# Windowed attention and a routed mixture of experts: when the experts' matrices are loaded, and where the flag of the leftover pass is made

## Chip, cores and metric

One core of a Trainium2 chip. The metric is the device time of one execution in microseconds (us); several runs are made and their median is taken. Beside the runs there is one profiled execution, from which all views below come. Engines: PE is TensorE's matmul stream and PEld its weight loads, DVE is VectorE, ACT is ScalarE, POOL is GpSimd, SP is SyncE, which here issues the direct DMAs.

## The reference

Two blocks follow each other. The first is attention with 4 batches, 8 heads, 768 positions and head size 64, where a query sees the first `n_global` positions and a window of `n_local` (96) behind it, with a slope per head on the distance. The second is a mixture of 8 experts over the 3072 rows of 512 that come out, and each row goes to one expert:

```python
xn = x / (np.linalg.norm(x, axis=-1, keepdims=True) + 1e-06)
en = expert_emb / (np.linalg.norm(expert_emb, axis=-1, keepdims=True) + 1e-06)
logits = xn @ en.T / tau
expert_idx = np.argmax(logits, axis=1)
...                                     # softmax of logits; gate_w = the chosen expert's share
for e in range(E):
    mask = expert_idx == e
    h = np.maximum(x[mask] @ w1[e], 0.0)        # 512 -> 1024
    out[mask] = gate_w[mask, None] * (h @ w2[e])   # 1024 -> 512
```

All is in float32.

## The kernel before

**Attention, 0 to about 190 us.** Batches and heads go through in steps that are written out by hand; rows of the result go to DRAM, each row's expert is chosen on the way, and row numbers are scattered into one list for each expert. Nothing of this is changed, but that two small DVE operations of the flag (below) stood here in the order before.

**Experts, about 190 us to the end.** The order on every engine is written out by hand. A first piece (256 rows of expert 0) is started early. Then comes a loop over experts `e` = 0 to 7:

- `prepare(e + 1)` issues on POOL the four gathers of the next expert's rows (`xg`, L986) and, from expert 2 on, on SP the loads of that expert's matrices: `load_weights` (L167 for `w1`, L168 for `w2`, 2 MB each). There are two sets of buffers, so `w1` of expert e + 1 goes where that of expert e - 1 was.
- The scatters of the expert before (`out_dram`, L1247) are issued on POOL, then a POOL drain waits for them to land.
- `expert(e)`: all engines branch (a `Switch`, L1752) into the arm for the expert's number of rows. Of those arms only one runs. Inside, `first_by_seven` makes the first product with seven half-size products instead of eight (L1295 on PE, sums by L1307 on DVE); between the products, `fill` calls put other DVE work: `wsum` from this expert's `w2` (L1040 to L1043, two and two), and `fsum` and in-place sums from the *next* expert's `w1` (L1065, L1066), and the next rows' token sums (L1040, L1041 on `xT`). The list `spare` says which work goes to which of the six fills. Between products PE also transposes the next expert's rows (L1012). Then come the rows over 256 (`part_in_arm` L1241, `second_in_arm` L1228).
- Behind the arm, `Pair` makes the second product of the first 256 rows with seven products (L1102): `begin` has four of them with fills behind the second, third and fourth, `end` the other three. `begin`'s fills hold the rest of the next expert's sums (L1042, L1043, L1067, L1068) and, on each engine, the load of a later expert's width into a register (`take_width`, L1498). A hint for the next branch is given ahead of it (L1504).

Waits around the loads: SP's first load of an expert waits not only for its buffer but also for `k.out_again`, an operation of the `Pair` two experts before the loaded one. That is the ACT copy of the first product (L1127), or for expert 2 a DVE operation of expert 0's `end_apart`:

```python
self.k.out_again = nc.scalar.copy(out=self.p1, in_=m).ins
...
t.w = new_weights(n, (wp_a, n.wp_b)[e % 2])
wait_for(n, load_weights(n, e, t.w), [n.out_again])
```

**The leftover.** After the loop, `leftover` makes two flags: whether inputs are outside what the window code can do, and whether any expert has more than 512 rows left. A product with ones on PE (L1516) and five DVE operations give the flag `fi`, all engines load it into a register (L1525) and branch (L1526) past a long, general pass that does not run with these inputs.

Of the kernel before, what the change touches and what calls it, by code (L numbers as in the profile page):

```python
# [9 lines left out]
F32 = mybir.dt.float32  # L10
I32 = mybir.dt.int32
AF = mybir.ActivationFunctionType
ALU = mybir.AluOpType
# [7 lines left out]
P = 128  # L21
NEG = 1e9
CAP = 512
# [141 lines left out]
def load_weights(k, e, w):  # L165
    nc = k.nc
    first = nc.sync.dma_start(w[0][:], k.w1[e].rearrange("(c p) f -> p c f", p=P))  # L167
    nc.sync.dma_start(w[1][:], k.w2[e].rearrange("(f p) m -> p f m", p=P))  # L168
    return first
# [915 lines left out]
class Pair:  # L1085
# [13 lines left out]

    def product(self, ps, x, w, add=False):  # L1100
        for f in range(4):
            self.k.nc.tensor.matmul(ps, lhsT=x[:, f, :], rhs=w[:, f, :], start=f == 0 and not add, stop=True,  # L1102
                                    skip_group_check=True)

    def plus(self, out, x, z):
        self.k.nc.vector.tensor_tensor(out=out, in0=x, in1=z, op=ALU.add)  # L1106
# [3 lines left out]

    def last(self, i, out, x, z):

        return self.k.nc.vector.scalar_tensor_tensor(out=out, in0=x, scalar=self.gate[i], in1=z, op0=ALU.mult, op1=ALU.add)

    def scatter(self, i):
        return lambda: scatter_rows(self.k, self.y[i][:], self.ids[:, i, 1:2])

    def begin(self, split=False, spare=((), (), ())):

        def fill(i):  # L1120
            for make in spare[i]:
                make()

        nc, (t1, t2, t3, t4), (s1, s2, s3, s4) = self.k.nc, self.sums, self.left
        m = self.m = self.bank()
        self.product(m, self.a[0][0], self.b[0][0])
        self.k.out_again = nc.scalar.copy(out=self.p1, in_=m).ins  # L1127
        n = self.bank()
        self.product(n, s2, t2)
        self.plus(self.u2, n, self.p1)  # L1130
        nc.scalar.mul(self.u2g, self.u2, self.gate[0])
        fill(0)
        if split:
            self.fourth()
        n = self.bank()
        self.product(n, s3, t3)
        self.plus(self.u3, n, self.u2)
        nc.scalar.mul(self.u3g, self.u3, self.gate[1])
        fill(1)
        n = self.bank()  # L1140
        self.product(n, self.a[1][1], t4)
        self.last(1, self.part(1, 0), n, self.u3g)
        fill(2)
# [20 lines left out]
    def end_apart(self):  # L1164

        t1, (s1, s2, s3, s4) = self.sums[0], self.left
        n = self.bank()
        self.product(n, s1, t1)
        self.k.out_again = self.last(1, self.part(1, 1), n, self.u3g).ins
        self.last(0, self.u3, n, self.u2g)  # L1170
        n = self.bank()
        self.product(n, s4, self.b[1][1])
        self.last(0, self.part(0, 1), n, self.u3)
        return [self.scatter(0), self.scatter(1)]
# [83 lines left out]
def wait_for(k, i, others):  # L1258
    for x in others:
        k.tc.add_manual_dep(i.ins, x.name,  # L1260
                            mybir.DependencyInfo(mybir.DependencyClass.Sync, mybir.DependencyReason.DATA),
                            reason="it comes behind all of them")
# [75 lines left out]
def expert(k, now, coming, widths, unfinished):  # L1338


    tc = k.tc
    w1, w2 = now.w
    hT = new_hidden(k)
    if coming:
        coming.xT = new_turned(k)

    def between(f):
        at = {1: (0,), 2: (1,), 3: (2,), 4: (3,)} if now.e else {5: (0,), 6: (1, 2), 7: (3,)}
        for j in at.get(f, ()) if coming else ():
            turn_row(k, coming.rows, coming.xT, j, k.nc.scalar.copy)  # L1350

    a = [[hT[:, 4 * j : 4 * j + 4, i * P : (i + 1) * P] for j in range(2)] for i in range(2)]
    now.sums, spare = weight_sums(k, w2)
    left, making = hidden_sums(k, a)
    more, ahead = [], []
    if coming:
        coming.token_sums, more = token_sums(k, coming.xT)
        if now.e:
            coming.first_sums, ahead = first_sums(k, coming.w[0])
    spare = [spare[:2], spare[2:], ahead[:1], ahead[1:2], more[:2], []]  # L1360
    tiles = range(2 if now.e else 1, CAP // P)
    ps = None if now.e else k.work0.tile([P, k.DM], F32, name="work", tag="work")
    k.order = list(range(4, 8)) + list(range(4)) if now.e else list(range(8))
    steps = widths_of(now.e)
    for arm in tc.Switch(now.width.index, len(steps), hint=now.width.hint):
        w = steps[arm]
        if now.e:
            first_by_seven(k, now, hT, w, between, list(spare))
            for make in making:
                make()  # L1370
        else:
            first_by_eight(k, now.xT, w1, hT, w, between)
        for size in (32, 64):
            if w % (2 * size) >= size:
                part_in_arm(k, now, hT, w2, w // (2 * size) * 2 * size, size)
        for j in tiles:
            if j < w // P:
                second_in_arm(k, now, hT, w2, j)
        if ps:
            second(k, ps, hT, w2, range(k.NF // 2))  # L1380

    def scatters():
        for j in tiles:
            scatter_rows(k, now.y[:, j - 1, :], now.tile_ids[:, j : j + 1])
        for size in (64, 32):
            scatter_rows(k, now.y_part[size][:], now.parts[size][0], P // size)

    def choose_next():
        if coming:
            give_hint(k, coming.e, widths[coming.e])  # L1390

    out = [scatters]
    if now.e:
        pair = Pair(k, now.rows, a, left, w2, now.sums)
        choose_next()
        out += unfinished.pop()()
        number = [lambda: widths.append(take_width(k, now.e + 2))] if now.e + 2 < k.E else []
        pair.begin(spare=(more[2:], number + ahead[2:3], ahead[3:]))
        ps = k.work0.tile([P, k.DM], F32, name="work", tag="work")
        unfinished.append(pair.end(ps[:, 0:256]))  # L1400
        out.append(pair.scatter(1))
    else:
        choose_next()
        widths.append(take_width(k, 2))
        out += unfinished.pop()()
        for make in more:
            make()
        second(k, ps, hT, w2, range(k.NF // 2, k.NF))
        unfinished.append(lambda: end_second(k, now.rows, ps))
    return out  # L1410
# [82 lines left out]
def take_width(k, e):  # L1493

    t = Net()
    n = len(widths_of(e))
    engines = ARMS if e else ARMS[:2]
    v = k.nc.values_load(k.pick[0:1, e : e + 1], engines=engines, min_val=0, max_val=n - 1)  # L1498
    t.index, t.hint = {eng: v for eng in engines}, "expert%d" % e
    return t  # L1500
# [3 lines left out]
    k.tc.switch_hint(t.index, len(widths_of(e)), t.hint)  # L1504


def leftover(k):


    nc, tc, E = k.nc, k.tc, k.E  # L1510
    passes = -(-k.N // CAP)
    more = passes - 1
    flags = k.const.tile([P, 2], F32, name="flags")
    ps = k.work.tile([P, 512], F32, name="work", tag="work")
    nc.vector.tensor_tensor(out=k.good[:], in0=k.good[:], in1=k.fits[:], op=ALU.mult)
    nc.tensor.matmul(ps[:, 0:1], lhsT=k.ones[:], rhs=k.good[:], start=True, stop=True)  # L1516
# [1 line left out]
                            op0=ALU.is_lt)  # L1518
# [1 line left out]
    nc.vector.tensor_reduce(out=most[:], in_=k.need[:], op=ALU.max, axis=AX.X)  # L1520
    nc.vector.tensor_scalar(out=flags[:, 1:2], in0=most[:], scalar1=float(CAP), scalar2=flags[:, 0:1],
                            op0=ALU.is_gt, op1=ALU.max)
    fi = k.const.tile([P, 2], I32, name="fi")
    nc.vector.tensor_copy(out=fi[:], in_=flags[:])
    any_ = nc.values_load(fi[0:1, 1:2], min_val=0, max_val=1)  # L1525
    with tc.If(any_ > 0):  # L1526

        wait_for(k, nc.sync.dma_start(k.i_dram[0:1, 0:2], fi[0:1, :]), k.outs)
        redo = nc.values_load(fi[0:1, 0:1], min_val=0, max_val=1)
# [7 lines left out]
        with ExitStack() as inner:  # L1537
# [15 lines left out]
            with tc.For_i(0, E * passes, 1) as i:  # L1553
# [3 lines left out]
                with tc.If(n > 0):  # L1557
                    e = i // passes
# [16 lines left out]
def kernel(  # L1575
# [13 lines left out]
    n = Net()  # L1589
# [26 lines left out]
    with ExitStack() as moe:  # L1616
# [43 lines left out]
        def prepare(e):  # L1660
            t = Net()
            t.e = e
            t.y, t.y_part = ys[e % 2]
            xgs, t.gathers = gather_rows(n, n.ids[:, e], n.xgp)
            t.rows = n.mt[:, e], n.ids[:, e], xgs
            if e < 2:
                t.w = n.w[e]
            else:
                t.w = new_weights(n, (wp_a, n.wp_b)[e % 2])
                wait_for(n, load_weights(n, e, t.w), [n.out_again])  # L1670
            return t

        with tc.manual_schedule(engines=ORDERED | set(ARMS) | {mybir.EngineType.Pool}):
# [37 lines left out]
            for e in range(n.E):  # L1711
                now, coming = coming, None
                parts_of(n, now)
                now.width = widths[e]
                if e == 1:
                    now.first_sums = first
                if e + 1 < n.E:
                    coming = prepare(e + 1)
                for scatter in pending:
                    scatter()  # L1720

                nc.gpsimd.drain()
                pending = expert(n, now, coming, widths, unfinished)
# [33 lines left out]
```

## Time and profile before

| | |
|---|---|
| Median of 5 runs | 523.28 us (521.61 to 524.31) |
| The profiled execution's own time | 523.07 us |
| Its span, first to last instruction | 521.3 us |
| PE busy | 497.4 us, 95% of the span |
| DVE, ACT, POOL busy | 302.4, 197.4, 152.0 us |
| Mean granted clock of PE | 0.99 |
| Instruction queue q8 | 63 packets, 1.03 MB |
| `w1t` loads of 2 MB | 6, landing 9.3 us after issue (median) |
| `w2t` loads of 2 MB | 6, landing 11.2 us after issue (median) |

The span lies inside the execution's time. "Idle before" in a row is the engine's own idle time ahead of an instruction, with the one that ended it; "issue" there means that the profile shows nothing that it waited for. A `q` behind an engine's name means its sequencer, which runs branches, register loads and waits. [...]

### The profile page before, as it was taken

The page shows a single profiled execution, that of the slowest core. Times are in us where ns is not written, and L with a number is a line of the kernel's source. Part 1 is how long each engine was busy: PE and PEld are TensorE (multiplying, and loading weights), DVE is VectorE, ACT ScalarE, POOL GpSimd, SP SyncE. Part 2 cuts the span into 40 slices and gives each one's busy share as a digit, 9 for nine tenths or more (in the row PEclk, how much of TensorE's full clock was granted, in tenths as well). Part 3 has the DMA queues.
Part 4 walks back from the last instruction along what each step waited for, and adds up shares of the span by engine and source line. Part 5 has one row for each costly group of instructions (what it writes and reads, how often), then busy time and mean ns, then how long its engine had stood idle before and what let it go on. Part 6 is the DMA issues. An engine that isn't in the chain of part 4 may idle for free.

```text
span 521.3 us, 13699 instructions
## 1 busy us (share of the span) xinstructions
PE 497.4 (95%) x5606; PEld 410.3 (79%) x5606; DVE 302.4 (58%) x601; ACT 197.4 (38%) x494; POOL 152.0 (29%) x169
## 2 busy tenths in 40 slices
PE   7999999999989898999989999999999999999994
PEld 6677787786767687788868669989899689869963
DVE  5656667776785665639625516746647554615531
ACT  4866776776744311313212221322323222311210
POOL 4221221152355335533430034054033040022031
PEclk9999999999998999999989999999999999999998
DMA  9999998988533627776480028257075073001002
GB/s 173 199 197 180 219 238 187 217 207 210 149 83 112 143 37 193 217 250 203 152 304 4 3 73 313 105 212 248 4 245 213 4 253 133 2 25 58 0 22 68
DMA packets 111422, 76.32 MB, mean 146 GB/s; under 512 B 87078, under 2 KB 95270, under 8 KB 111282
## 3 DMA queue, kind: packets, MB, share of 16 engines
q1 hardware_dynamic: 102769, 59.00, 42.9%
q0 software_dynamic: 6912, 15.26, 9.1%
q8 instruction: 63, 1.03, 0.9%
q14 instruction: 78, 0.63, 0.4%
q10 hardware_dynamic: 1600, 0.39, 0.3%
HBM read 61.66 MB, written 17.16 MB: 151 GB/s over the span
## 4 chain that ended last, share of the span: by engine, by line
PE 80%; DVE 5%; issue 4%; ACT 4%; DMA 3%; POOL 2%; SPq 1%; POOLq 0%; ACTq 0%; DVEq 0%
PE big L1295 24%; PE big L1102 13%; PE work L1228 7%; PE od L509 6%; PE work L1102 5%; PE pa L480 4%; PE work L1241 4%; PE pa L455 3%; PE od L519 3%; PE pa L671 2%; PE work L1012 2%; ACT ex L486 2%; PE big L1271 2%; PE pa L582 1%; PE pa L559 1%
## 5 line engine op out<-in xcount | busy, mean ns | idle before, releaser
L493 DVE TENSOR_TENSOR ex<-ex,table 126x768 f32<-126x768 f32 x64 | 61.0, 959 | 39.5 <-ACT ex L486 39.2
L1307 DVE TENSOR_TENSOR hT<-big,hT 128x320 f32<-128x320 f32 (+4 forms) x70 | 39.2, 565 | 44.6 <-PE big L1295 44.3
L1247 POOL DMA_INDIRECT out_dram<-y_arm,tids x17 | 17.0, 1002 | 162.2 <-ACT y_arm L1230 121.8
L1295 PE MATMUL big<-xT,w1t 128*128 128x160 f32 (+4 forms) x336 | 61.0, 335 | 2.3 <-issue 2.3
L1295 PEld LDWEIGHTS big<-xT,w1t 128*128 128x128 f32 x336 | 55.3, 193 | 5.5 <-issue 3.2
L486 ACT ACTIVATE ex<-pa 126x384 f32<-126x384 f32 (+1 forms) x128 | 53.1, 477 | 16.1 <-PE pa L480 15.0
L986 POOL DMA_INDIRECT xg<-x_dram,idss x32 | 34.9, 1089 | 51.0 <-PE big L1295 16.7
L509 PE MATMUL od<-ex,v 126*64 126x192 f32 (+1 forms) x576 | 46.8, 308 | 0.0
L509 PEld LDWEIGHTS od<-ex,v 126*64 126x64 f32 x576 | 35.0, 138 | 7.7 <-issue 3.8
L1295 PE MATMUL big<-xsum,fsum 128*128 128x160 f32 (+4 forms) x224 | 39.7, 330 | 1.2 <-DVE hT L1307 1.2
L1015 ACT COPY xT<-work 128x256 f32<-128x256 f32 x56 | 18.0, 376 | 56.5 <-PE work L1012 56.1
L257 POOL DMA_INDIRECT meta<-mt,slot x24 | 27.2, 1135 | 37.9 <-DVE rd L553 18.4
L480 PEld LDWEIGHTS pa<-qT,kT 64*32 64x32 f32 (+1 forms) x2048 | 29.3, 105 | 11.4 <-issue 6.7
L1295 PEld LDWEIGHTS big<-xsum,fsum 128*128 128x128 f32 x224 | 36.1, 190 | 2.5 <-DVE hT L1307 1.4
L480 PE MATMUL pa<-qT,kT 64*32 64x128 f32 (+3 forms) x2048 | 37.7, 264 | 0.2
L1228 PE MATMUL work<-w2t,hT 128*128 128x512 f32 x80 | 35.1, 594 | 0.0
L430 POOL COPY v<-v 30x896 f32<-30x896 f32 (+1 forms) x15 | 18.3, 1230 | 51.4 <-DMA v<-in_v_dram 15.3
L1102 PE MATMUL big<-wsum,hsum 128*128 128x256 f32 x136 | 31.1, 380 | 1.1 <-PE work L1022 0.6
L1309 ACT ACTIVATE hT<-hT 128x320 f32<-128x320 f32 (+4 forms) x42 | 21.7, 533 | 25.0 <-DVE hT L1307 24.9
L1102 PEld LDWEIGHTS big<-wsum,hsum 128*128 128x128 f32 x136 | 25.7, 190 | 5.7 <-issue 1.4
L1228 PEld LDWEIGHTS work<-w2t,hT 128*128 128x128 f32 x80 | 15.1, 190 | 17.7 <-issue 17.6
L1106 DVE TENSOR_TENSOR ptmp<-big,ptmp 128x256 f32<-128x256 f32 x16 | 6.8, 422 | 37.6 <-PE big L1102 37.2
(245 smaller groups left out, 898.1 us busy)
## 6 DMA issues: line engine op xcount, KB each, us to landing
w1t<-in_moe_w_dram SPq DMA_DIRECT2D x6, 2048.0 KB, 9.3
w2t<-in_moe_w_dram SPq DMA_DIRECT2D x6, 2048.0 KB, 11.2
v<-in_v_dram SPq DMA_DIRECT2D x32, 192.0 KB, 4.7
x_dram<-xs SPq DMA_DIRECT2D x23, 256.0 KB, 3.2
k<-in_k_dram SPq DMA_DIRECT2D x28, 192.0 KB, 4.7
q<-in_q_dram SPq DMA_DIRECT2D x28, 192.0 KB, 4.5
w1t<-in_moe_w_dram SPq DMA_DIRECT2D x32, 128.0 KB, 4.6
w2t<-in_moe_w_dram SPq DMA_DIRECT2D x32, 128.0 KB, 5.0
```

Of the source, the lines that this page charges most:

```text
L257: i = nc.gpsimd.indirect_dma_start(out=k.meta[:], out_offset=bass.IndirectOffsetOnAxis(ap=slot[:, t : t + 1], axis=0), in_=mt[:, t, :], in ...
L480: i = nc.tensor.matmul(u.sp[e][k0:k1, a * n + c0 : a * n + c1], lhsT=t.kT[rows, j, k0:k1], rhs=t.qT[rows, j * BLK + c0 : j * BLK + c1], st ...
L486: nc.scalar.activation(u.ex[:, e], u.sp[e][0:ROWS, 0 : 2 * u.n].rearrange("p (a c) -> p a c", a=2), AF.Exp, scale=k.scale)
L493: nc.vector.tensor_tensor(out=exv, in0=exv, in1=tab[:, :, 0 : u.n // BLK, :], op=ALU.mult)
L509: nc.tensor.matmul(g.od[a][e * D : (e + 1) * D, at : at + c1 - c0], lhsT=g.v[0:ROWS, 2 * a + e, u.j, :], rhs=u.ex[:, e, a, c0:c1], start=f ...
L986: i = k.nc.gpsimd.indirect_dma_start(out=xg[:], out_offset=None, in_=k.x_dram[0 : upto or k.N + 1, :], in_offset=bass.IndirectOffsetOnAxis ...
L1102: self.k.nc.tensor.matmul(ps, lhsT=x[:, f, :], rhs=w[:, f, :], start=f == 0 and not add, stop=True, skip_group_check=True)
L1228: nc.tensor.matmul(ps[:], lhsT=hT[:, f, j * P : (j + 1) * P], rhs=w2[:, f, :], start=i == 0, stop=i == k.NF - 1)
L1241: nc.tensor.matmul(ps[i * size : (i + 1) * size, 0:m], lhsT=hT[:, f, base : base + size], rhs=w2[:, f, i * m : (i + 1) * m], start=o == 0, ...
L1295: nc.tensor.matmul(to[f // 2][:, f % 2 * 256 : f % 2 * 256 + h], lhsT=x[:, l, f * P : (f + 1) * P], rhs=y[:, l, 0:h], start=not (add or f ...
L1307: nc.vector.tensor_tensor(out=to, in0=x, in1=z, op=ALU.add)
L1309: nc.scalar.activation(to, to, AF.Relu)
```

## The change

Five edits:

1. The loads move from `prepare(e + 1)` to behind the scatters in the loop's text. SP has no scatters, so its order stays; what changes is the wait. Expert 2's load waits for the last scatter of expert 0 to land (`n.outs[-1]`).
2. `out_again` is now the last matmul of `Pair.begin`'s first product, for the loads of experts 3 to 7, and no longer ACT's copy of it. `product` returns it.
3. For expert 1 the fills move: nothing at the third, L1065 at the fourth, L1066 and the first token sum at the fifth, the second token sum at the sixth.
4. The flag's operations (`flag_leftover`) are made at expert 2, in the last fill of `Pair.begin`, behind the last `fsum` step. On PE the flag's matmul stands between the fourth and the fifth product of the `Pair`; on DVE its five operations stand behind L1068 (L1068 in both kernels).
5. All engines load the flag into a register (`load_flag`) at expert 6, where there is no width left to load. `leftover` keeps the branch alone.

On the other engines' queues the order is otherwise the same; on POOL the register load comes ahead of expert 6's scatters, on SP behind the load of expert 7's `w2`. Lines behind the edits are 1 to 17 higher in the changed kernel (L1295 is L1296, L1307 is L1308, L1516 is L1520, L1247 is L1248).

```diff
     def product(self, ps, x, w, add=False):
         for f in range(4):
-            self.k.nc.tensor.matmul(ps, lhsT=x[:, f, :], rhs=w[:, f, :], start=f == 0 and not add, stop=True,
-                                    skip_group_check=True)
+            i = self.k.nc.tensor.matmul(ps, lhsT=x[:, f, :], rhs=w[:, f, :], start=f == 0 and not add, stop=True,
+                                        skip_group_check=True)
+        return i.ins
...
-        self.product(m, self.a[0][0], self.b[0][0])
-        self.k.out_again = nc.scalar.copy(out=self.p1, in_=m).ins
+        self.k.out_again = self.product(m, self.a[0][0], self.b[0][0])
+        nc.scalar.copy(out=self.p1, in_=m)
...
-        self.k.out_again = self.last(1, self.part(1, 1), n, self.u3g).ins
+        self.last(1, self.part(1, 1), n, self.u3g)
...
     spare = [spare[:2], spare[2:], ahead[:1], ahead[1:2], more[:2], []]
+    if now.e == 1:
+        spare[2:6] = [], ahead[:1], ahead[1:2] + more[:1], more[1:2]
...
         number = [lambda: widths.append(take_width(k, now.e + 2))] if now.e + 2 < k.E else []
+        if now.e == k.E - 2:
+            number.append(lambda: load_flag(k))
+        if now.e == 2:
+            ahead.append(lambda: flag_leftover(k))
...
+def flag_leftover(k):
+
+    nc = k.nc
+    k.flags = flags = k.const.tile([P, 2], F32, name="flags")
     ps = k.work.tile([P, 512], F32, name="work", tag="work")
     nc.vector.tensor_tensor(out=k.good[:], in0=k.good[:], in1=k.fits[:], op=ALU.mult)
     nc.tensor.matmul(ps[:, 0:1], lhsT=k.ones[:], rhs=k.good[:], start=True, stop=True)
...
+    nc.vector.tensor_copy(out=k.fi[:], in_=flags[:])
+
+
+def load_flag(k):
+    k.any = k.nc.values_load(k.fi[0:1, 1:2], min_val=0, max_val=1)
...
-    any_ = nc.values_load(fi[0:1, 1:2], min_val=0, max_val=1)
-    with tc.If(any_ > 0):
+    fi, flags = k.fi, k.flags
+    with tc.If(k.any > 0):
...
-                wait_for(n, load_weights(n, e, t.w), [n.out_again])
...
                 for scatter in pending:
                     scatter()
+                if e and coming:
+                    wait_for(n, load_weights(n, e + 1, coming.w), [n.outs[-1] if e == 1 else n.out_again])
```

More of the change, by code (lines that the diff above doesn't have):

```diff
@@ L1111, in last @@
     def last(self, i, out, x, z):
-        return self.k.nc.vector.scalar_tensor_tensor(out=out, in0=x, scalar=self.gate[i], in1=z, op0=ALU.mult, op1=ALU.add)
+        self.k.nc.vector.scalar_tensor_tensor(out=out, in0=x, scalar=self.gate[i], in1=z, op0=ALU.mult, op1=ALU.add)
     def scatter(self, i):
@@ L1504, in give_hint @@
     k.tc.switch_hint(t.index, len(widths_of(e)), t.hint)
[L1507 to L1513, printed above, removed]
+def flag_leftover(k):
+    nc = k.nc
+    k.flags = flags = k.const.tile([P, 2], F32, name="flags")
     ps = k.work.tile([P, 512], F32, name="work", tag="work")
@@ L1522, in leftover @@
                             op0=ALU.is_gt, op1=ALU.max)
[L1523 to L1526, printed above, removed]
+    k.fi = k.const.tile([P, 2], I32, name="fi")
+    nc.vector.tensor_copy(out=k.fi[:], in_=flags[:])
+def load_flag(k):
+    k.any = k.nc.values_load(k.fi[0:1, 1:2], min_val=0, max_val=1)
+def leftover(k):
+    nc, tc, E = k.nc, k.tc, k.E
+    passes = -(-k.N // CAP)
+    more = passes - 1
+    fi, flags = k.fi, k.flags
+    with tc.If(k.any > 0):
         wait_for(k, nc.sync.dma_start(k.i_dram[0:1, 0:2], fi[0:1, :]), k.outs)
```

## The prediction

> **What bounds the kernel now.** I read the page first, then the chain of waits in order of time, then the timeline and stage tables around each piece that the diff touches. Busy time and the chain agree: TensorE (PE) is the bound, 95% busy and 80% of the chain.
>
> ```profile
> span 521.3 us, 13699 instructions
> PE 497.4 (95%) x5606; PEld 410.3 (79%) x5606; DVE 302.4 (58%) x601; ACT 197.4 (38%) x494; POOL 152.0 (29%) x169
> PE 80%; DVE 5%; issue 4%; ACT 4%; DMA 3%; POOL 2%; SPq 1%; POOLq 0%; ACTq 0%; DVEq 0%
> ```
>
> So an edit counts where PE stands still in the expert stage, or in the tail after its last product. The chain (start, duration, what) shows two such places before expert 3:
>
> ```profile
> 228.34 5.61 issue
> ...
> 235.35 1.22 DVE wsum L1041
> 236.57 0.41 DVE hT L1307
> 236.98 0.04 issue
> 237.02 2.44 PE big L1295 x16
> ...
> 262.75 2.31 issue
> 265.06 8.70 PE big L1295 x32
> ```
>
> First: VectorE (DVE) takes expert 1's branch at 228.26 and does nothing for 5.61 us, though expert 1's second matrix was issued by 213.0; PE pays 1.16 us, waiting for L1307 (235.87 to 237.02). Second: PE itself is idle for 2.31 us on entering expert 2, waiting for nothing but its branch:
>
> ```profile
> L1752 PEldq COMPARE_BRANCH  x1: 4572/4572/4572, 260.2 to 260.2; - x1
> ```
>
> This branch took 4572 ns; nine PE branches between 300 and 480 us took 298 to 316 ns. The stage table (window, length, busy time of PE, PEld, DVE, ACT, POOL, granted clock, DMA share, GB/s) adds a second price:
>
> ```profile
> 152.17:155.58 3.41, 1.50 (x21) 1.14 (x21) 2.41 (x14) 1.42 (x5) 1.76 (x2) 1.00 0.16 26
> 234.09:237.50 3.41, 2.25 (x17) 2.02 (x17) 3.29 (x5) 1.32 (x4) 0.90 (x1) 1.00 1.05 405
> 261.40:264.81 3.41, 1.35 (x7) 0.84 (x5) 0.95 (x1) 0.14 (x1) 0.13 (x1) 1.00 0.71 184
> 264.81:268.22 3.41, 3.16 (x8) 2.56 (x9) 1.41 (x2) 0.00 (x0) 1.70 (x2) 0.50 0.99 357
> ```
>
> After 3.41 us with PE busy 1.35 us the clock is halved for the next 3.41 us; the rows behind the other two (not shown) grant 0.50 after 1.50 us busy and 1.00 after 2.25. Expert 2's first sixteen matmuls took 5.25 us, the next sixteen 3.62: 1.63 us lost. The second stall costs 2.31 + 1.63 = 3.94 us in all.
>
> **Part 1, expert 2's load behind expert 0's last scatter.** Now w1 is issued at 223.86 and w2 at 228.50, and the queues run at 400 GB/s from 231 to 236, where DVE's code should come. DVE's idle time ahead of its first wsum is 5.87 us here, but 2.66 at expert 7, with no load under way, and 3.28 at expert 3. The last scatter starts at 227.32 and lands only 7.9 us later under this traffic; a quiet one takes 2.7 (that at 511.63). So w1 would be issued near 230.5, after DVE's code has come, and DVE starts near 231.5 instead of 234.2. The two wsum (1.22 each) and L1307 then end before 235.87: I take the whole 1.16 us; bounds 0.5 and 1.2. Behind SP's new wait stand w2 and later loads. Who needs them: L1065 of expert 1 reads w1. w1 landed 9.3 us after issue for expert 4, 11.3 for expert 2, so 239.8 to 241.8; the fills are moved later by one product, and L1065 falls behind the sixth L1307, near 241.5. At 9.3 it is free; at 11.3 DVE is 0.3 us late, less than the half microsecond to a whole one that stands between L1307 and its reader L1241. At worst (gathers for expert 3, now in the same traffic, add 2 us) PE waits 1.5 us. I take 0.
>
> **Part 2, other first matrices behind the product instead of ACT's copy.** For expert 3 the copy (L1127) ran at 253.50 because ACT was late, and w1 went out at 253.90; the product ended at 252.2. The load comes 1.6 us earlier, besides the 1.16 of part 1. Its 7.7 us of traffic then end near 259, before PE's code for expert 2 is asked for (1 to 2 us after a branch at 259.0), not at 261.6, beside it. A PE branch that misses took 3665 ns at 223.0 and 3780 at 495.9, both with little traffic: I take 3.65, a gain of 0.92 (bounds 0 and 1.2). The idle time becomes 1.4 us; 1.16 left the clock alone, 1.91 (at 152.3) did not, and 1.4 is nearer to the former: 1.63 more. Elsewhere the loads come 0.4 to 2.5 us earlier and PE does not wait for them: 0.
>
> **Part 3, the flag at expert 2.** In PE's order the flag's matmul (L1520) stands behind the fourth product and ahead of the last three, and waits for DVE, which does the fsum step L1068 before the flag's first operation. The timeline of expert 2:
>
> ```profile
> 311.72 1.89 PE L1102 MATMUL big<-wsum,hT 128*128 128x256 f32 x8
> 313.45 1.89 PE L1102 MATMUL work<-wsum,hsum 128*128 128x256 f32 x8
> 313.71 0.48 DVE L1113 SCALAR_TENSOR_TENSOR y<-big,mts,ptmp 128x256 f32<-128x256 f32 x1
> 314.11 1.21 DVE L1068 TENSOR_TENSOR fsum<-w1t,fsum 128x1024 f32<-128x1024 f32 x1
> ```
>
> L1068 ends at 315.32, the flag's multiplication (0.15) at about 315.4. PE, which would go on at 313.45, goes on after the flag's two weight loads and two matmuls (0.2 each pair, tail rows of L1516 before): 315.45 + 0.6 - 313.45 = 2.6 us lost; bounds 2.0 (loads pulled ahead) and 2.9. Nothing hides it, since PE is the bound and later products queue behind. The idle piece is 2.0 us, so whether the clock is halved depends on how it falls on the 3.41 us grid: with 1.5 to 1.9 us needed inside one window, 0.5 to 0.75 of the positions do it, at 1.7 us. By the rows: 2.6 or 4.3.
> [...] The rows above show a drop after 2.31 us of idle time, so I let the rows decide.
>
> DVE's four other flag operations (0.15 to 0.21 each) lie beside these products, with L1106 next behind them at least 1 us later: 0. The register load at expert 6 (five engines, 0.3 to 0.5 us each) stands where other experts load their width without a gap on PE; on POOL it is ahead of expert 6's scatters, on SP behind its last load: 0.
>
> **Part 4, the tail.** Before, the end is this (chain, then SP's wait):
>
> ```profile
> 514.71 0.18 DVE fi L1524
> 514.88 0.03 issue
> 514.92 0.50 POOLq L1525
> 515.42 0.68 POOL out_dram L1247
> SPq L1526 <- SPq L1526: 3.4, 1, 3.4
> ```
>
> All five engines branch at 515.3 to 515.6 and then wait 2.9 to 4.3 us for code; SP follows with 1.5 us of semaphores and 0.8 of closing barrier. The last scatter starts 0.78 us after its DVE operation instead of 0.28, and lands 4.4 us later instead of 2.7. With the flag in registers SP branches after expert 6 and PE before its last products end; the scatter starts at 514.65, 0.5 earlier, lands between 517.4 and 519.0, and 1.6 us of SP's and POOL's closing follow: 519.0 to 520.6 instead of 521.3, or 0.7 to 2.3. I take 1.6, nearer to the quiet landing.
>
> **The sum.** The profiled execution took 523.07 (span 521.27 and 1.80 around it), 0.2 below the median of 523.28. 523.07 - 1.16 - 0.92 - 1.63 - 1.6 + 2.6 = 520.4; with the clock halved behind the flag's wait 522.1. [...] A median over runs that fall on either side lies between, and I forecast the middle: 521.2.
>
> **Rivals.** *The entrance of expert 2 stays as it is*: PE's branch still misses with as much traffic, 0.92 and 1.63 are not gained: 523.8, no change. For it: the branch's code is the same, and scatters of expert 1 still move 0.25 MB each at that time. Against: both misses with little traffic were 0.8 us shorter. 0.20.
> *A new miss* (slower): expert 2's tail has four more TensorE instructions, so all later PE code moves; one of the five entrances that now take 0.3 us misses instead, at 2.31 + 1.63 = 3.9: 525.1. It decides from the first miss on. For it: two of seven entrances miss now. Against: four instructions are little beside the blocks in which code arrives (63 packets for 1.03 MB in the page's instruction queue). 0.08.
> *The flag's wait spares the clock and the tail gives all*: 520.4 - 0.7 = 519.7, faster. 0.10.
> The forecast has 0.62.
>
> **How the numbers follow.** About 0.3% of 523.28, 1.6 us, is what a measurement can tell: faster means below 521.7. The forecast's own range is 520.3 to 522.1 with 0.72 of it below 521.7: 0.45; with the third rival's 0.10, about 0.54. Slower is the new miss, 0.08; the rest, 0.38, is no change. The range takes the third rival below and the unchanged entrance above, leaving out the new miss: 519.4 to 523.8.
>
> **What would show it.** DVE's gap before expert 1 at 2.7 to 3.5 us and no idle PE before its L1295; PE's gap at expert 2 at 1.0 to 1.8 us, its first sixteen matmuls at 3.6; a PE wait of about 2.0 us on DVE ahead of L1520; the last scatter starting 0.3 us after DVE, and the end 5.5 us or less behind it. Wrong would make it: L1065 of expert 1 waiting for w1t, a PE branch of several microseconds after expert 2, or no PE gap at L1520.

## The result, and the profile after

The changed kernel takes 521.69 us (median of 52 runs, 519.5 to 526.95) against 523.31 for the kernel before on the same chips (94 runs). The ratio is 0.9971, with a 95% interval of 0.9960 to 0.9983: 1.6 us less, and 0.5 us above the forecast. A second comparison on another chip gave 0.9975 (0.9951 to 0.9999).

The profiled execution took 523.28 us, which is 1.6 above the median of its kernel, with a span of 521.5. So what was gained is read stage by stage, not from the two spans. The page's first lines:

```profile
span 521.5 us, 13699 instructions
PE 499.5 (96%) x5606; PEld 411.4 (79%) x5606; DVE 301.2 (58%) x601; ACT 197.4 (38%) x494; POOL 147.5 (28%) x169
```

The counts of instructions are those of before. The chain of waits in order of time (start, duration, what) goes through every place that the prediction named:

```profile
229.41 4.35 PE big L1296 x32
233.76 0.44 PE work L1012 x4
234.20 2.17 PE big L1296 x16
...
262.33 1.81 issue
264.14 7.15 PE big L1296 x32
...
304.05 7.10 PE big L1102 x32
311.15 0.04 DVEq L1114
311.19 0.04 issue
311.23 0.48 DVE y L1114
311.71 1.13 DVE fsum L1068
312.85 0.08 DVE good L1519
312.93 0.04 issue
312.97 0.38 PE work L1520 x2
313.36 2.80 PE work L1102 x8
316.16 2.45 PE big L1102 x8
318.60 1.73 PE work L1102 x8
```

Expert 1's first products now run on PE without a stop: no DVE piece stands between them in the chain, where the kernel before had L1041 and L1307. The entrance of expert 2 costs 1.81 us instead of 2.31, and the 32 matmuls behind it take 7.15 instead of 8.70. Then comes what the change added: PE ends the fourth product at 311.15 and goes on with the fifth at 313.36, 2.21 us later, behind DVE's L1114, L1068 and the flag's multiplication. The two products behind it take 2.80 and 2.45 us, where the next of eight matmuls takes 1.73 (granted clock 1.00 from 317.49 on): 1.79 us more. The table of stages (window, length, busy time of PE, PEld, DVE, ACT, POOL, granted clock, DMA share, GB/s) shows the clock:

```profile
310.66:314.07 3.41, 1.57 (x9) 1.09 (x8) 2.73 (x8) 0.00 (x0) 1.25 (x1) 1.00 1.00 401
314.07:317.49 3.42, 3.42 (x10) 2.71 (x9) 0.43 (x2) 0.47 (x1) 0.09 (x1) 0.50 0.29 117
```

PE was busy 1.57 of 3.41 us and then had 0.50 granted for the next 3.42. PE's branches, from the list of all (least, median, longest in ns, first and last start) and from that of 255 to 270 us:

```profile
L1769 PEldq COMPARE_BRANCH  x16: 298/314/4067, 205.1 to 497.4; - x16
L1769 PEldq COMPARE_BRANCH  x1: 4067/4067/4067, 259.7 to 259.7; - x1
```

DVE's first wsum of expert 1 and the last scatter, from the timelines, first of the kernel before and then of the changed one:

```profile
234.21 1.23 DVE L1040 TENSOR_TENSOR wsum<-w2t 128x1024 f32<-128x1024 f32 x1 [5.87 <-issue]
...
513.87 0.48 DVE L1113 SCALAR_TENSOR_TENSOR y<-work,mts,u2g 128x256 f32<-128x256 f32 x1 [2.52 <-PE work L1102]
...
515.13 0.98 POOL L1247 DMA_INDIRECT out_dram<-y,idss  x1 [2.52 <-DVE fi L1524]
```

```profile
232.30 1.23 DVE L1040 TENSOR_TENSOR wsum<-w2t 128x1024 f32<-128x1024 f32 x1 [3.02 <-issue]
...
515.46 0.48 DVE L1114 SCALAR_TENSOR_TENSOR y<-work,mts,u2g 128x256 f32<-128x256 f32 x1 [2.52 <-PE work L1102]
516.72 0.98 POOL L1248 DMA_INDIRECT out_dram<-y,idss  x1 [2.52 <-ACTq L1542]
```

The longest branch is the one into expert 2: 4067 ns where it was 4572. DVE is idle for 3.02 us ahead of expert 1's first wsum, where it was 5.87. In the tail the last scatter starts 0.78 us after DVE's operation ends, exactly as before (513.87 + 0.48 to 515.13), but lands at 519.90, 3.2 us after its start instead of 4.4. In the kernel before it landed at 519.57, and at the same time PE and SP were through with the branch past the leftover pass: PE's took 4260 ns from 515.3, and SP went through nine semaphores behind its own up to 519.6 (from the list of that line):

```profile
L1526 SPq EVENT_SEMAPHORE  x9: 17/17/17, 519.0 to 519.6; - x9
...
L1526 PEldq COMPARE_BRANCH  x1: 4260/4260/4260, 515.3 to 515.3; - x1
```

So a shorter landing alone could have gained next to nothing there, as the branch had to be over earlier too. In the changed kernel it is: SP waits for the landing from 516.5 on.

### The profile page after: what moved, and what is told of

Read it like the earlier page. It is cut to its first block, busy times and chain, and to the rows that moved or that the text cites. A ratio compares the mean times of both kernels' runs of the same rounds, so it can differ in the third digit from the quotient of the medians.

```text
span 521.5 us, 13699 instructions
## 1 busy us (share of the span) xinstructions
PE 499.5 (96%) x5606; PEld 411.4 (79%) x5606; DVE 301.2 (58%) x601; ACT 197.4 (38%) x494; POOL 147.5 (28%) x169
## 4 chain that ended last, share of the span: by engine, by line
PE 64%; issue 4%; DVE 3%; POOL 2%; DMA 1%; ACT 0%; POOLq 0%; DVEq 0%
PE big L1296 25%; PE big L1102 14%; PE work L1229 7%; PE work L1102 5%; PE work L1242 4%; PE work L1012 2%; PE pa L671 2%; PE big L1272 2%; PE work L1022 1%; DMA meta<-mt,slot 1%; POOL ss L224 1%; POOL meta L257 1%; POOL xg L986 0%; DVE xT L1015 0%; PE od L519 0%
## 5 line engine op out<-in xcount | busy, mean ns | idle before, releaser
L1308 DVE TENSOR_TENSOR hT<-big,hT 128x320 f32<-128x320 f32 (+4 forms) x70 | 39.4, 566 | 51.0 <-PE big L1296 50.7
L1248 POOL DMA_INDIRECT out_dram<-y_arm,tids x17 | 17.0, 1001 | 169.4 <-ACT y_arm L1231 121.7
L1296 PE MATMUL big<-xT,w1t 128*128 128x160 f32 (+4 forms) x336 | 59.4, 330 | 1.8 <-issue 1.8
L1296 PEld LDWEIGHTS big<-xT,w1t 128*128 128x128 f32 x336 | 54.2, 190 | 4.5 <-issue 2.7
L986 POOL DMA_INDIRECT xg<-x_dram,idss x32 | 32.1, 1002 | 44.0 <-PE big L1296 22.5
L1296 PE MATMUL big<-xsum,fsum 128*128 128x160 f32 (+4 forms) x224 | 39.6, 330 | 0.0
L1296 PEld LDWEIGHTS big<-xsum,fsum 128*128 128x128 f32 x224 | 36.1, 190 | 1.1
L430 POOL COPY v<-v 30x896 f32<-30x896 f32 (+1 forms) x15 | 16.7, 1123 | 50.1 <-DMA v<-in_v_dram 29.3
L1102 PE MATMUL big<-w2t,hT 128*128 128x256 f32 x112 | 28.4, 393 | 0.0
```

The source lines that it names most:

```text
L986: i = k.nc.gpsimd.indirect_dma_start(out=xg[:], out_offset=None, in_=k.x_dram[0 : upto or k.N + 1, :], in_offset=bass.IndirectOffsetOnAxis ...
L1102: i = self.k.nc.tensor.matmul(ps, lhsT=x[:, f, :], rhs=w[:, f, :], start=f == 0 and not add, stop=True, skip_group_check=True)
L1296: nc.tensor.matmul(to[f // 2][:, f % 2 * 256 : f % 2 * 256 + h], lhsT=x[:, l, f * P : (f + 1) * P], rhs=y[:, l, 0:h], start=not (add or f ...
L1308: nc.vector.tensor_tensor(out=to, in0=x, in1=z, op=ALU.add)
```

## The experiments

The runs were made on several chips, on which the kernel before took 523 to 531 us, so ratios to it on the same chip are compared, and beside them stages. The table has, from each profile: **A**, from expert 1's first L1295 (L1296) to PE's end ahead of expert 2; the gap there; **D**, from expert 2's first to expert 3's first product; the tail from PE's last matmul to the end (where the flag is made at the end, that is the flag's, 0.11 us behind the last product); and all from expert 1's first product to the end. From expert 3's first product to PE's last matmul it takes 195.2 to 195.6 us in all of them. A star marks a profile in which the clock was halved in D.

| kernel | A | gap | D | tail | to the end | ratio (95%) |
|---|---|---|---|---|---|---|
| before | 34.44 | 2.31 | 53.57* | 7.32 | 292.96 | 1 |
| before_once_more | 34.21 | 2.01 | 52.01 | 7.41 | 290.94 | |
| before_third_profile | 34.89 | 2.58 | 53.69* | 7.42 | 293.88 | |
| expert2_load_alone | 33.02 | 2.46 | 52.01 | 7.39 | 290.36 | 0.9964 (0.9936 to 0.9991) |
| other_loads_alone | 34.35 | 1.35 | 52.01 | 7.33 | 290.33 | 0.9973 (0.9946 to 1.0000) |
| loads_moved_flag_at_end | 33.14 | 1.56 | 52.01 | 7.34 | 289.36 | 0.9932 (0.9903 to 0.9961) |
| flag_alone | 34.58 | 0.36 | 54.33 | 6.07 | 290.88 | 1.0009 (0.9974 to 1.0043) |
| changed | 33.08 | 1.81 | 56.02* | 6.06 | 292.23 | 0.9971 (0.9960 to 0.9983) |
| changed_once_more | 33.02 | 1.59 | 56.02* | 6.07 | 292.23 | 0.9975 (0.9951 to 0.9999) |
| flag_wait_doubled | 33.02 | 1.56 | 55.59 | 6.01 | 291.81 | 1.0005 (0.9972 to 1.0038) |
| flag_ready_early | 33.04 | 1.46 | 52.23 | 6.08 | 288.00 | 0.9916 (0.9892 to 0.9941) |
| flag_ready_early_again | 33.02 | 1.65 | 52.23 | 6.20 | 288.74 | 0.9895 (0.9859 to 0.9931) |
| flag_early_expert3_load_later | 33.10 | 1.64 | 52.23 | 6.00 | 288.60 | 0.9906 (0.9871 to 0.9941) |
| fills_not_moved | 33.02 | 1.49 | 52.23 | 6.08 | 288.18 | 0.9894 (0.9861 to 0.9928) |

The theory: the loads' order gains at expert 1 and at the entrance of expert 2, the early branch gains in the tail, and the flag's wait on PE, with a halved clock behind it in some executions, takes most of that back. The rivals: one part does all; or the flag's wait is covered and costs nothing.

**Loads moved, flag at the end.** The changed kernel without its flag part:

```diff
-        if now.e == k.E - 2:
-            number.append(lambda: load_flag(k))
-        if now.e == 2:
-            ahead.append(lambda: flag_leftover(k))
...
+def leftover(k):
...
+    nc.vector.tensor_copy(out=fi[:], in_=flags[:])
+    any_ = nc.values_load(fi[0:1, 1:2], min_val=0, max_val=1)
+    with tc.If(any_ > 0):
```

> The changed kernel with the flag made and loaded behind the last expert, as before; loads and fills stay changed. Theory (the loads give 1.5 us at expert 1 and 0.5 at the entrance of expert 2, and 1.6 more where the clock is not halved behind it; the flag is a separate loss): 2.0 to 3.6 us below the kernel before, 519.7 to 521.3 us; no idle PE in expert 1, a PE branch of about 4.1 us and a PE gap of about 1.8 at expert 2, none between the fourth and the fifth product of expert 2, and the last scatter landing 4.4 us after its start as before. Rival (the loads' order brings nothing, all of the gain is the tail's): the time of the kernel before, 523.3.

It came out at 0.9932, which is 3.6 us of 523.3, better than the whole change. Expert 2's seven products follow each other without a gap:

```profile
307.20 7.09 PE big L1102 x32
314.29 1.73 PE work L1102 x8
316.02 1.73 PE big L1102 x8
317.75 1.73 PE work L1102 x8
```

So the gain is the loads', and the flag part as it stands is a loss: by the profiles 2.87 us, of which 1.69 are the halved clock (by the ratios alone the two would not be told apart, as their intervals just meet). The rival that the tail does it all falls.

**The flag alone.** The kernel before with only `flag_leftover` at expert 2 and `load_flag` at expert 6 (the added lines of the diff above).

> The kernel before with the flag alone moved: made at expert 2, loaded at expert 6; loads and fills as before. Theory (PE waits 2.2 us behind DVE's fsum step, half of the time with 1.8 more of halved clock, and the tail gives 1.4): 0.8 to 2.6 us above the kernel before, 524.1 to 525.9; a PE gap of about 1.8 us ahead of the flag's matmul and about 6 us from the last product's end to the end of the span. Rival (the wait is made good later in expert 2, where products wait for DVE and ACT anyway, so that the flag is a gain): 1.4 us below it, 521.9.

The ratio 1.0009 excludes the rival's 0.9973 only just, but the stages are plain: D is 54.33 against 52.01, 2.32 more, and the tail 6.07 against about 7.4, 1.3 less. The cost is not made good later in the expert. The chain shows DVE, not PE, ahead of the flag:

```profile
316.32 1.13 DVE fsum L1068
317.45 0.08 DVE good L1516
317.53 0.04 issue
317.57 0.38 PE work L1517 x2
317.96 1.83 PE work L1102 x8
```

Behind the flag's matmul the granted clock was 1.00 here, and the next eight matmuls took 1.83 us. This profile has the shortest entrance of all, 0.36 us: PE's branch took 2689 ns, and a 16 KB packet of the instruction queue started 0.13 us after it, where in the other thirteen profiles it was 0.9 to 2.2 us. Why is not known; the load for expert 3 was under way then as in the kernel before (394 GB/s in the microsecond before the branch and 410 in the next).

**The flag's multiplication early.** In the changed kernel, the one DVE operation that PE's matmul waits for is put two fills ahead, in front of both fsum steps:

```diff
+        if now.e == 2:
+            more.append(lambda: flag_good(k))
         pair.begin(spare=(more[2:], number + ahead[2:3], ahead[3:]))
...
+def flag_good(k):
+    k.nc.vector.tensor_tensor(out=k.good[:], in0=k.good[:], in1=k.fits[:], op=ALU.mult)
...
-    nc.vector.tensor_tensor(out=k.good[:], in0=k.good[:], in1=k.fits[:], op=ALU.mult)
     nc.tensor.matmul(ps[:, 0:1], lhsT=k.ones[:], rhs=k.good[:], start=True, stop=True)
```

> The changed kernel with the flag's first DVE operation (the multiplication that PE's matmul waits for) two fills earlier, behind the second product of expert 2 and ahead of the fsum steps; all else as changed. Theory (PE waits for nothing but that operation): 1.8 us less than the changed kernel, and up to 3.6 less where the clock was halved behind the wait: 518.1 to 519.9; no PE gap over 0.3 us between the fourth and the fifth product of expert 2, which costs 0.4 us for its two matmuls. Rival (the wait only moves: the products behind it then wait for DVE's later steps): 521.2 or more, with a new PE gap in the last three products of expert 2.

The chain at the same place:

```profile
308.76 7.09 PE big L1102 x32
315.85 0.12 PE work L1525 x2
315.96 1.83 PE work L1102 x8
317.80 1.73 PE big L1102 x8
```

The flag costs 0.22 us in D (52.23 against 52.01) instead of 2.32, no new wait comes behind it, and no clock is halved (1.83, 1.73 and 1.73 us for the three products of eight matmuls). The ratio of 0.9916 is 4.4 us of 523.3. It was run again beside the changed kernel on one chip:

> The kernel of flag_ready_early again, for a comparison with the changed kernel on one chip. Theory: 2.1 us less than the changed kernel, ratio to the kernel before 0.9935, and 42.9 us for the rest of expert 2. Rival (its first result was the chip's noise): the time of the changed kernel.

> The changed kernel, profiled and timed again beside the next kernels. Theory (1.5 us from expert 1, 0.7 from the entrance of expert 2, 1.3 from the tail, 2.3 lost at the flag): ratio to the kernel before 0.9975, stages as in its first profile (34.7 us for expert 1 up to PE's end, gap of 1.4 to 1.8 us at expert 2, 45 us for the rest of expert 2, 6.05 at the end), and the halved clock behind the flag's wait, 1.8 us in the first profile, comes only by the chance of where the wait falls. Rival (the halved clock belongs to the flag's wait): it comes again, and expert 2's rest takes 46 us or more.

There the medians were 525.18 (523.08 to 528.64) against 528.63 (526.74 to 530.16) and 530.36 for the kernel before: this version beats both. The changed kernel repeated its stages to 0.1 us, but for a gap of 1.59, and the halved clock behind the flag came again. So the theory held on the flag's cost and underestimated how much the early multiplication brings, 3.45 us between the medians and not 2.1. Between the two profiles it is 3.49 us from expert 1 on, and the halved clock, which only the changed kernel's has, is 1.69 of that.

**The flag's wait doubled.** The last fsum step of expert 2 is made twice, with the same result:

```diff
-            ahead.append(lambda: flag_leftover(k))
+            ahead += [ahead[3], lambda: flag_leftover(k)]
```

> The changed kernel with the last fsum step of expert 2 (L1068, 1.13 us on DVE) made twice, the second time with the same result, so that the flag's multiplication and PE's matmul come that much later. Theory (each microsecond of DVE work ahead of the flag's matmul is a microsecond of PE): the gap grows from 1.84 to about 3.0 us, the time by 1.1 to 1.2, and the clock is halved behind it more often, for 1.7 us each time: ratio to the kernel before 0.999 to 1.003, against 0.9971 of the changed kernel. Rival (PE's wait is covered later in the expert): the ratio stays at 0.997.

The ratio, 1.0005, is inside the theory's. PE's gap ahead of the flag's matmul became 3.09 us and D 3.58 above its value without the flag, 1.26 more than with one step (flag_alone), for a step that takes DVE 1.2: DVE's work ahead of the matmul is PE's time, one for one. But the longer wait was *not* followed by a halved clock. The tables of stages of this kernel and of flag_alone show where the waits fell:

```profile
309.76:313.17 3.41, 2.01 (x10) 1.42 (x8) 3.28 (x5) 0.51 (x1) 2.60 (x2) 1.00 0.92 353
313.17:316.59 3.42, 1.73 (x9) 1.58 (x10) 2.21 (x7) 0.00 (x0) 0.00 (x0) 1.00 0.72 287
316.59:320.00 3.41, 3.41 (x18) 3.00 (x17) 0.42 (x1) 0.95 (x2) 0.98 (x1) 1.00 0.07 22
```

```profile
313.09:316.50 3.41, 2.65 (x13) 1.99 (x11) 3.24 (x6) 0.78 (x2) 2.80 (x3) 1.00 0.96 330
316.50:319.92 3.42, 2.35 (x12) 2.12 (x13) 1.63 (x6) 0.09 (x1) 0.13 (x1) 1.00 0.96 386
```

The drops of the clock lie on a grid: in the profile before they begin at 155.58, 264.81 and 517.40, which is 32 and 74 times 3.413 us apart, and in that of the changed kernel at 157.06, 314.07 and 518.87, which is 46 and 60 times. Both gaps here fall across a border of the grid, so that neither window lost more than 1.7 us. In both profiles of the changed kernel the gap lay whole inside one window, with 1.57 and 1.59 us busy, and the clock was halved. That is a pattern of four profiles, not a test: where a wait falls could not be set.

**Expert 2's load alone, and the other loads alone.** The first has the load behind the last scatter and the moved fills, with ACT's copy kept for the others; the second has only this:

```diff
-        self.product(m, self.a[0][0], self.b[0][0])
-        self.k.out_again = nc.scalar.copy(out=self.p1, in_=m).ins
+        self.k.out_again = self.product(m, self.a[0][0], self.b[0][0])
+        nc.scalar.copy(out=self.p1, in_=m)
```

> The kernel before with expert 2's load behind the last scatter of expert 0, and expert 1's fills moved as in the change; the other loads wait for ACT's copy and the flag stays at the end. Theory: 1.2 to 1.5 us below the kernel before (521.8 to 522.1), with no idle PE in expert 1 and DVE idle 3.2 us there; the entrance of expert 2 keeps its PE branch of 4.2 to 4.6 us. Rival (DVE's code is late for another reason than the traffic): the gap of 1.16 us stays, 523.3. Second rival (expert 1's end comes so much earlier that the load for expert 3 clears the entrance too): 520.2, with a PE branch under 4.0 us.

> The kernel before with one edit: the loads of experts 3 to 7 wait for TensorE's product and not for ACT's copy of it. Expert 2's load, the fills and the flag are as before. Theory: w1 of expert 3 goes out 0.4 to 1.6 us earlier, PE's branch at expert 2 gets its code 0.3 to 1 us earlier, and the time falls by as much: 522.3 to 523.0 on the scale of 523.3, a ratio of 0.998 to 0.9995; expert 1 keeps its PE gap of about 1.2 us. Rival (the entrance of expert 2 varies by itself, from 0.36 to 2.46 us in the profiles so far, and the edit does nothing): ratio 1.000 and a PE gap at expert 2 of 2.3 us or more.

They are cleanly apart. The first has A at 33.02 with DVE idle only 2.86 us, and keeps the gap at the entrance:

```profile
238.28 1.23 DVE L1040 TENSOR_TENSOR wsum<-w2t 128x1024 f32<-128x1024 f32 x1 [2.86 <-issue]
```

```profile
268.41 2.46 issue
270.87 7.14 PE big L1295 x32
```

The second keeps expert 1's wait for DVE, with A at 34.35, and has the short entrance (chain; the interval of its ratio, 0.9973, takes in the theory's and the rival's, so the stages decide):

```profile
236.34 1.22 DVE wsum L1041
237.56 0.41 DVE hT L1308
237.97 0.04 issue
238.02 2.44 PE big L1296 x16
...
263.75 1.35 issue
265.09 7.14 PE big L1296 x32
```

So in these profiles each edit works at its own place, and the second rival of the first run, one edit for both, falls. Against the rival that the entrance varies by itself stand all the profiles: 1.35 to 1.81 in the nine with the product, 2.01 to 2.58 in four of the five with ACT's copy, but 0.36 in the fifth, flag_alone.

**Expert 3's load later too.** On top of flag_ready_early, expert 3's load also waits for the last scatter ahead of it, and expert 2's fills move as expert 1's do:

```diff
-    if now.e == 1:
+    if now.e in (1, 2):
...
-                    wait_for(n, load_weights(n, e + 1, coming.w), [n.outs[-1] if e == 1 else n.out_again])
+                    wait_for(n, load_weights(n, e + 1, coming.w), [n.outs[-1] if e in (1, 2) else n.out_again])
```

> As flag_ready_early, and expert 3's load too waits for the last scatter of the expert before it, with expert 2's fills moved as expert 1's are. Theory (PE's code for expert 2 comes late because of the load's traffic): with no load under way the branch at expert 2 takes 3.7 us and the gap stays at 1.4 to 1.5, as the code itself takes that long; so no gain over flag_ready_early where its load had already landed by then, and DVE's and ACT's code come 0.1 to 0.3 us earlier: ratio 0.991 to 0.993. Rival 1 (the traffic still mattered): the gap falls under 1.0 us and the ratio below 0.991. Rival 2 (the load is now too late): L1065 of expert 2 waits for w1t and PE loses 0.5 to 2 us, ratio 0.993 to 0.996.

The load was issued at 263.74, after PE's branch was over, and the gap is 1.64, no shorter than with the load from 257 on. So with the load's traffic out of the way the branch is no shorter (3979 ns here, 3677 to 4067 in the eight others with the product), and moving the load still later gained nothing. That the 1.4 to 1.6 us of idle PE which are left are the code itself, as the theory has it, is not shown: in flag_alone the branch took 2689 ns. The ratio, 0.9906, is one with flag_ready_early. L1065 found its data in time.

**Fills not moved.** flag_ready_early without the two lines that move expert 1's fills:

```diff
-    if now.e == 1:
-        spare[2:6] = [], ahead[:1], ahead[1:2] + more[:1], more[1:2]
```

> flag_ready_early with expert 1's fills where they were before the change, so that L1065, which reads w1 of expert 2, is asked for behind the third product and not behind the fourth. Theory (w1 lands 9 us after an issue about 4.1 us behind expert 1's first matmul, at 13.1 us, and DVE comes to L1065 some 10 us behind it): DVE waits about 2.5 us for w1t, its sums come late, and PE stands still for 1 to 2 us in expert 1, which takes 35.7 to 36.7 us instead of 34.7; ratio 0.9955 to 0.9975. Rival (the sums have that much slack): expert 1 takes 34.7 us as with the moved fills, and the ratio is that of flag_ready_early.

The rival is right. DVE does wait for w1, but only 1.13 us, as w1 landed 8.9 us after its issue:

```profile
249.99 1.23 DVE L1065 TENSOR_TENSOR fsum<-w1t 128x1024 f32<-128x1024 f32 x1 [1.13 <-DMA w1t<-in_moe_w_dram]
```

A is 33.02 all the same, and the ratio 0.9894. The moved fills gain nothing in this case: the wait of 1.13 us is not passed on to PE.

**The kernel before, two more profiles.**

> The kernel before, profiled a second time. Theory, by the four profiles since: the stages of the experts repeat within 0.3 us (36.2 us for expert 1 up to PE's end, 42.7 for expert 2 behind its first 32 matmuls, 7.3 from PE's last product to the end), the gap at the entrance of expert 2 lies between 1.9 and 2.5 us, and the halved clock behind it, which cost 1.6 us in the profile before, is a matter of where the gap falls on the 3.41 us grid and need not come again. Rival (the halved clock follows from a gap over 2 us): it comes again, with 8.5 us for the first 32 matmuls instead of 7.0.

> The kernel before, profiled a third time, since the comparisons gave each changed kernel about 1 to 2 us more than its stages save against before_once_more. Theory (in the kernel before, the clock is halved behind the entrance of expert 2 in most executions, and before_once_more was one of the others): the first sixteen matmuls of expert 2 take 5.1 us again, and expert 1's first product to the end takes 292.5 to 293. Rival (the halved clock is the exception, and the difference lies ahead of the experts): 3.5 us and 290.5 to 291.5.

On the clock both came as their theories say: the first had no halved clock (3.5 us for the sixteen matmuls, 290.9 to the end), the second had it (5.2, and 293.9 to the end, 0.9 above the theory's range). The second's gap of 2.58 us, at whose end DVE's first wsum was late too, lies in one window:

```profile
268.40:271.81 3.41, 0.83 (x4) 0.59 (x4) 1.90 (x2) 0.00 (x0) 0.00 (x0) 1.00 0.59 183
271.81:275.23 3.42, 3.42 (x10) 2.71 (x9) 0.46 (x1) 0.59 (x1) 2.21 (x3) 0.50 1.04 381
```

That is two of three profiles, too few for a share. The mean granted clock of the timed executions gives a bound, as an estimate: in 11 of 72 of the kernel before it was 0.996 or more, which leaves at most 4.7 us of 522 at half clock, as the profiles of before and changed show no grants but 1.00 and 0.50. The end of the span alone had 2.9 to 3.9 in the three profiles, so those 11 can hardly have had a window of 3.41 us at half clock ahead of it. And one window speaks against a plain rule: in expert2_load_alone PE was busy 1.48 us of 3.41 and the clock stayed.

## Why the prediction was right, and which of its terms were off

The sign and the mechanism came as forecast: two stalls shortened, one wait added, a shorter tail. The time came 0.5 us from the forecast, in part by luck, since its terms were off both ways: the gains of the clock at expert 2 and of the tail were too large by 0.5 and 0.3, the gain of part 1 was too small by 0.3, and the flag's loss too large by 0.3. By its own steps:

- **Part 1, 1.16 us.** Five profiles without the edit have A at 34.2 to 34.9 (mean 34.5), all with it 33.0 to 33.1: 1.4 us. The PE gap was 0.92 to 1.60 in them and is gone; the rest is the next sixteen matmuls, 2.44 us behind the wait and 2.17 without, a term that the sum left out. That L1065 would be free was right, with the moved fills and also without them.
- **Part 2, 0.92 us at the entrance.** The gaps were 2.01 to 2.58 with ACT's copy (four profiles, mean 2.34, the 0.36 of flag_alone left out) and 1.35 to 1.81 with the product (eight, flag_early_expert3_load_later left out; mean 1.56): 0.78. With flag_alone the copy's mean is 1.94 and the term 0.39, so its size hangs on that one profile. The first profile alone showed only 0.50: its load was still landing (260.77) when PE's branch had begun (259.74). The sum had 7.7 us for the load's traffic, but w1 landed 8.4 us after its issue in the kernel before and 8.8 in the changed one, so it did not end near 259.
- **No halved clock behind it, 1.63 us.** True of the profiled execution, but not of the median: the kernel before had it in two of three profiles, and the nine profiles with the product in none. As a term for the median it is about 1.1, an estimate from these three (two thirds of 1.63).
- **The flag, 2.6 us.** 2.32 in D (flag_alone), of which 0.22 remain when DVE is ready early. The two pairs of weight loads and matmuls were put at 0.6 and took 0.38 in the chain.
- **The clock behind the flag, 1.7 us in half to three quarters of the cases.** 1.79 by the chain and 1.69 by D (56.02 less 54.33) where it came, and it came in two of the four profiles that have the wait, both of the changed kernel. That the changed kernel is also spared at times shows in its executions' mean granted clock: 19 of 54 have 0.997 or more, by the same estimate at most 3.7 us at half clock, and the end of the span had at least 0.6 of that in every profile, so no whole window of 3.41 us is left for the flag. The middle that the forecast took for a median over both cases is borne out in that, though the share is not known. The 1.5 to 1.9 us taken as needed inside one window were an estimate from the 1.16 and 1.91 of the profile before; 1.93 us of idle PE in one window left the clock alone in expert2_load_alone (1.48 us busy of 3.41).
- **The tail, 1.6 us.** 1.3. The step that failed: the last scatter did not start 0.5 earlier. The 0.78 us between DVE's operation and POOL's start are there without any register load between them, so the register load was not their cause. The end came earlier by the landing, 3.2 us instead of 4.4, and because SP and PE no longer came out of the leftover's branch as late as the landing; what shortened the landing was not separated.

Summed with these sizes: -1.4 - 0.8 - 1.1 + 2.3 + 0.9 - 1.3 = -1.4 us, and measured were -1.6 (-0.9 to -2.1). The stages of the better version give 288.4 on the mean of the four profiles with the early multiplication against 292.6 for the three profiles of before: -4.2, and -4.4 was measured the first time, -5.5 the second (-3.6 to -7.4).

Of the rivals, "the entrance stays as it is" is against the gaps, of which only flag_alone's stands out; "a new miss" did not come, as PE's branches into experts 3 to 7 take 290 to 402 ns in all fourteen profiles; "the flag's wait spares the clock" is right of some executions and wrong of others, and the tail did not give all.

On the clock the rows show 0.50 granted behind windows in which PE was busy 0.83, 1.35, 1.57 and 1.59 us of 3.41 (before_third_profile, before, changed, changed_once_more). A wait of 1.83 or 1.84 us cost 1.7 us more inside one window (both profiles of the changed kernel) and nothing across a border (flag_alone).

What stays open: what makes the clock drop, since 1.48 us busy once left it alone, and elsewhere 0.50 came behind 1.89 us (before_once_more, 202 to 206 us) while 1.58 left it alone (flag_wait_doubled, 170 to 173 us), so the busy time of one window alone does not decide it; how often it drops in the kernel before, as three profiles are few; and why flag_alone's branch was so short.

## What to carry to other kernels

When a small job is moved from the end into the busy part, look at the one engine that must not wait: PE's matmul for the flag was nearly free (0.2 us), but it was queued behind DVE's fsum step, which made it ten times as dear. Put the producer of its operand early. When a profile shows a stall followed by a halved clock, count the stall in full and the clock by its chance, and profile the kernel before more than once, as an accident of one execution enters the sum as if it were the kernel's.

## What the runs showed of the hardware

- Behind a wait of 3.09 us the granted clock stayed 1.00 (flag_wait_doubled), behind one of 1.84 us it was 0.50 (changed): in these profiles the position on the 3.41 us grid told more than the length.
- Inside each branch of PE into expert 2 a 16 KB packet of the instruction queue comes in. It started 1.8 to 2.2 us after the branch in the four profiles with ACT's copy and the long gap, where the queues still moved 365 to 426 GB/s in the second microsecond behind the branch, and 0.9 to 1.5 us after it in the nine with the earlier or much later load, where they moved 25 to 49. flag_alone, with 0.13 us and 352 GB/s, does not fit, so the load's traffic is not the whole cause. PE's branch ended 1.4 us behind the end of the packet (263.33 to 264.72 before, 262.38 to 263.80 changed); that it waits for code is the author's reading, and was not shown.
- Another branch became longer where a load was moved beside it: PE's branch 18 to 20 us behind expert 1's first product took 312 ns in all five profiles with expert 2's early load, and 0.81 to 1.36 us in all nine with the later one, whose w2 was still landing then (in the changed kernel the branch began at 247.8 and w2 landed at 250.33). PE lost nothing by it, as A shows.
- For expert 2 in the changed kernel the two loads of 2 MB were issued 0.5 us apart (232.08 and 232.58) and did not land half a microsecond apart: w1 landed 9.0 us after its issue, and w2 17.8 us after its own.
